# Weights decoded in tile pairs by three bit operations, with a late range check and a new order of the first three unit pairs

## The chip, the cores and the metric

The kernel runs on one core of a Trainium2 chip. The metric is the device time of one execution in microseconds. The engines are TensorE (PE, with its weight loads PEld), VectorE (DVE), ScalarE (ACT), GpSimd (POOL) and SyncE (SP), whose queue issues all transfers of this kernel.

## What is computed

A gated linear attention with a complex diagonal decay feeds a two-layer network. Shapes: batch 4, heads 8, sequence 768, head width 48; the network maps 3072 rows of 384 to 2048 and back.

```python
mag = sqrt(a_re**2 + a_im**2)
scale = minimum(mag, 0.999) / (mag + 1e-6)
a_re_n, a_im_n = a_re * scale, a_im * scale
for t in range(S):
    new_re = ar * S_re - ai * S_im
    new_im = ar * S_im + ai * S_re
    S_re, S_im = new_re + outer(k[t], v[t]), new_im
    y[t] = q[t] @ S_re
x = y.transpose(0, 2, 1, 3).reshape(B * S, H * D)
h = x @ w_in
out = (h - tanh(h)) @ w_out
```

All inputs are float32 but the two weight matrices, which arrive as float64 and lie in memory as 64-bit words.

## The kernel before, in words

The sequence is cut into 6 chunks of 128 positions. A unit is one batch entry in one chunk (24 units); a unit pair g (12 of them, two batch entries of one chunk) is what the network works on: 256 rows. Letters name the steps. Gates: B, b, C, D, E (`gates_b` to `gates_e`) turn the decays of a pair into scale factors and rotations, with Ln, Exp, Arctan and Sin on ACT. `p` (`products`) scales and rotates q and k of one unit, splits them into two f16 parts and has them transposed by a DMA (the first four units work in f32 and are transposed by PE). `a` (`attention`) is the unit's attention: scores, mask, the state Z, and at the end `x16`, which a DMA transposes into `xT`.

Network: `head(g, fp)` multiplies `xT` of pair g with two of the 16 column tiles of w_in (18 matmuls of 256 columns, L521), takes tanh on ACT and h − tanh(h) on DVE into `mt`. `split` writes it as two f16 parts into `mg`. `tail(g, fp)` multiplies these with two tiles of w_out (12 matmuls of 384 columns, L548) into two accumulators; after the eighth, ACT copies them into an `io` tile (L552) and a DMA writes the result. A tail follows its head by LAG = 4 heads; 8 heads make a stage.

Weights: `decode` (L172 to L191) loads one tile of 384 64-bit words per partition (384 KB) into one of four `io` buffers, views it as low and high 32-bit words, each with a step of 8 bytes, and builds from them a float32 with a shifted exponent in `wtmp`: DVE shifts the low word (L181), ACT multiplies the high word as a float by a power of two into the low word's place (L184, shown as L112), DVE merges sign and top exponent bit (L185) and the rest (L186). ACT copies it to f16 (`dechi`), DVE subtracts that for the low half (`declo`). This runs once for each of 32 tiles. `weight_stats` squares both high halves of a tile on ACT and sums them; `check_stats` at the end compares these sums and other statistics with limits, and a kernel in general arithmetic runs if one is broken. Helpers record most instructions, so they show L102 (and L112, L119) in the trace.

Order of the work: START is the list of steps before the first head; FIRST, SECOND and CYCLE list, for pair 0, pair 1 and all others, which step stands at which of 16 half-steps of a stage. `i3` decodes tile 3 of w_in, `o3` of w_out, `q0` loads q, k, v of a unit, `p2` is a piece of products of unit 2g + 2, `w0` the weight statistics. EARLY (pairs 0 and 1) and OFFSET (later) shift the priority of each kind of instruction; a scheduler at build time orders each engine's queue by priority among what is ready in its own model, and the engines then run their queues in order.

Of the kernel before, what the change touches and what calls it, by code (L numbers as in the profile page):

```python
# [11 lines left out]
I32 = mybir.dt.int32  # L12
# [74 lines left out]
def tile_fast(ctx: ExitStack, tc: tile.TileContext, flag, a_in, qkv_in, win_in, wout_in, sq_c, vec_c, lim_c, out):  # L87
# [30 lines left out]
    def combine(which, kind, **k):  # L118
        by_name[ENGINE[which]](kind).tensor_tensor(**k)  # L119
# [52 lines left out]
    def decode(ft, kinds=(0, 1)):  # L172
        for kind in kinds:
            src = (win_in, wout_in)[kind]
            raw = sb.tile([P, 2, DM], F32, name="io", bufs=BUFS["io"]).rearrange("p two n -> p (two n)").bitcast(I32).rearrange("p (n two) -> p n two", two=2)
            SP("dec").dma_start(out=raw, in_=src[:, ft].bitcast(I32).rearrange("p (n two) -> p n two", two=2))
            tmp = sb.tile([P, DM], I32, name="wtmp", bufs=BUFS["wtmp"])
            lo, hi = raw[:, :, 0], raw[:, :, 1]
            top = raw.rearrange("p n two -> p (n two)").bitcast(U8).rearrange("p (n e) -> p n e", e=8)[:, :, 3]
            if ENGINE[f"lsb{kind}"] == "V":  # L180
                V("dec").tensor_scalar(out=tmp, in0=lo, scalar1=29, scalar2=None, op0=ALU.logical_shift_right)  # L181
            else:
                A("dec").activation(out=tmp, in_=top, func=AF.Copy, scale=1.0 / 32, bias=-0.484375)
            copy("base", "dec", lo.bitcast(F32), hi.bitcast(F32), 2.0 ** (-112 + SW // 8))  # L184
            V("dec").scalar_tensor_tensor(out=tmp, in0=hi, scalar=-1073741824, in1=tmp, op0=ALU.bitwise_and, op1=ALU.bitwise_or)  # L185
            V("dec").scalar_tensor_tensor(out=tmp, in0=lo, scalar=3, in1=tmp, op0=ALU.logical_shift_left, op1=ALU.bitwise_or)  # L186
            w = tmp.bitcast(F32)
            t = const.tile([P, 2, DM], F16, name=f"w{kind}_{ft}")
            (wi, wo)[kind][ft] = t
            copy("dechi", "dechi", t[:, 0], w)  # L190
            combine("declo", "declo", out=t[:, 1], in0=w, in1=t[:, 0], op=ALU.subtract)  # L191
# [389 lines left out]
    def step(g, x):  # L581
# [241 lines left out]
```

## Time and profile before

| | us |
|---|---|
| median of 3 runs | 574.05 (572.24 to 576.78) |
| span of the profiled execution, first to last instruction | 575.1 |
| PE, DVE, ACT busy in it | 504.1, 474.7, 473.0 |

The profile shows one execution, whose page gives its span; no other time of that execution is given. Its span is 1.05 us above the median. Times in rows are us from the start of the span; durations of single instructions are ns where a row says mean.

### The profile page before, as it was taken

Reading aid. Unit: us, or ns where it says so; the run is one execution under the profiler, and the core shown is the slowest. Engines: PE = TensorE matmul, PEld = TensorE weight load, DVE = VectorE, ACT = ScalarE, POOL = GpSimd, SP = SyncE. Lnnn points to the kernel's source line nnn. Section 1 sums busy time; section 2 is a strip of 40 time slices with the busy share of each in tenths; the row PEclk is TensorE's granted clock in tenths of the full one; section 3 lists DMA queues with packets and bytes.
Section 4 is the critical chain, followed back from the end, with each engine's and each line's share of the span. In section 5 each row is a group of like instructions: output and inputs, shape, how many; then the busy total and the mean of one; then the engine's idle time right before and its main releaser. Section 6 shows DMA issues by size and latency. Waiting matters only on the chain.

```text
span 575.1 us, 12672 instructions
## 1 busy us (share of the span) xinstructions
PE 504.1 (88%) x5058; PEld 387.7 (67%) x5058; DVE 474.7 (83%) x806; ACT 473.0 (82%) x951; POOL 2.1 (0%) x8
## 2 busy tenths in 40 slices
PE   2336499987699998999998999999999999999995
PEld 0125387865467876877776777778778777777773
DVE  4898899978799898898997998998998989853331
ACT  6978889897997998998988998998989989553551
POOL 1000000000000000000000000000000000000000
PEclk9859589998799999999998999999999999999998
DMA  7757744409757368267285285293582652720001
GB/s 229 229 165 172 244 135 107 129 14 175 152 93 153 98 103 175 67 134 166 56 152 135 57 169 147 67 184 104 100 178 65 135 110 56 146 59 15 2 27 33
DMA packets 133902, 68.12 MB, mean 118 GB/s; under 512 B 119982, under 2 KB 123694, under 8 KB 133836
## 3 DMA queue, kind: packets, MB, share of 16 engines
q1 hardware_dynamic: 133836, 67.25, 50.0%
q8 instruction: 41, 0.67, 0.5%
q14 instruction: 25, 0.20, 0.1%
HBM read 36.76 MB, written 4.78 MB: 72 GB/s over the span
## 4 chain that ended last, share of the span: by engine, by line
PE 35%; ACT 27%; DVE 21%; DMA 8%; issue 7%; SPq 0%; ACTq 0%; DVEq 0%
PE h L521 11%; PE o L548 11%; PE att L102 9%; ACT L102 5%; ACT a_raw L102 4%; DMA qT<-q 4%; DVE qkf L390 3%; DVE g_t L102 3%; DVE qkv_raw L387 2%; ACT mt L102 2%; ACT mg L102 2%; DVE q L119 2%; ACT g_t L102 2%; DVE mg L102 2%; DVE mt L102 2%
## 5 line engine op out<-in xcount | busy, mean ns | idle before, releaser
L521 PE MATMUL h<-xT,w 128*128 128x256 f16 x1728 | 208.3, 274 | 11.2 <-DMA xT<-x 8.9
L548 PE MATMUL o<-w,mg 128*128 128x384 f16 x1152 | 205.6, 328 | 4.4 <-ACT io L102 2.9
L521 PEld LDWEIGHTS <-w 128*128 128x128 f16 x1728 | 168.2, 98 | 40.8 <-DMA xT<-x 7.2
L548 PEld LDWEIGHTS <-mg 128*128 128x128 f16 x1152 | 111.8, 98 | 69.6 <-issue 4.6
L102 DVE SCALAR_TENSOR_TENSOR mt<-h,mt 128x512 f32<-128x512 f32 x96 | 64.9, 685 | 25.9 <-ACT mt L102 25.8
L102 DVE SCALAR_TENSOR_TENSOR mg<-mt,mg 128x512 f16<-128x512 f32 x96 | 65.1, 686 | 16.1 <-ACT mg L102 15.8
L102 ACT ACTIVATE mg<-mt 128x512 f16<-128x512 f32 x96 | 58.8, 624 | 22.1 <-DVE mt L102 21.9
L102 ACT ACTIVATE mt<-h 128x512 f32<-128x512 f32 x96 | 55.2, 586 | 20.5 <-PE h L521 19.9
L102 ACT ACT_TABLE_LOAD x39 | 50.0, 1283 | 1.4 <-PEq L816 0.8
L102 PE MATMUL att<-qT,kT 96*128 96x128 f16 (+1 forms) x544 | 41.8, 231 | 3.1 <-DMA kT<-k 2.5
L390 DVE TENSOR_TENSOR qkf<-qkv_raw,g_trig 128x768 f32<-128x768 f32 x44 | 41.0, 950 | 0.0
L102 ACT ACTIVATE a_raw<-a_raw 128x768 f32<-128x768 f32 (+2 forms) x49 | 38.9, 796 | 0.5 <-DVE a_raw L102 0.5
L102 PEld LDWEIGHTS <-kT 96*128 96x128 f16 x480 | 30.2, 101 | 6.1 <-DMA kT<-k 3.1
L102 DVE TENSOR_TENSOR a<-af,a 128x512 f16<-128x512 f32 x40 | 27.3, 685 | 7.7 <-ACT a L102 7.5
L102 DVE TENSOR_TENSOR af<-att,sqc 128x512 f32<-128x512 f32 x40 | 27.3, 687 | 6.5 <-PE att L102 5.3
L102 ACT ACTIVATE a<-af 128x512 f16<-128x512 f32 x40 | 24.9, 623 | 3.7 <-DVE af L102 3.7
L102 DVE SCALAR_TENSOR_TENSOR g_t<-g_t,a_raw 128x768 f32<-128x768 f32 (+1 forms) x26 | 23.2, 894 | 2.3 <-ACT a_raw L102 2.3
L102 ACT ACTIVATE w<-wtmp 128x384 f16<-128x384 f32 x32 | 16.0, 514 | 8.4 <-DVE wtmp L186 8.4
L102 ACT ACTIVATE g_trig<-g_t 128x768 f32<-128x768 f32 (+1 forms) x26 | 20.3, 785 | 2.9 <-DVE g_t L102 2.2
L102 ACT ACTIVATE g_t<-att 128x384 f32<-128x384 f32 x24 | 10.7, 485 | 13.8 <-PE att L219 13.8
L119 DVE TENSOR_TENSOR q<-qkf,q 128x768 f16<-128x768 f32 x20 | 19.1, 955 | 3.5 <-ACT q L102 3.4
L102 PE MATMUL att<-sqc,qkf 128*96 128x128 f32 x32 | 7.0, 386 | 16.1 <-DVE qkf L390 15.7
(94 smaller groups left out, 706.7 us busy)
## 6 DMA issues: line engine op xcount, KB each, us to landing
qkv_raw<-in_qkv SPq DMA_DIRECT2D x24, 576.0 KB
a_raw<-in_a SPq DMA_DIRECT2D x22, 384.0 KB
io<-in_win SPq DMA_DIRECT2D x16, 384.0 KB
io<-in_wout SPq DMA_DIRECT2D x16, 384.0 KB
out_dram<-io SPq DMA_DIRECT2D x24, 192.0 KB
a_raw<-in_a SPq DMA_DIRECT2D x4, 192.0 KB
xT<-x SPq DMA_TRANSPOSE x24
hd<-hscr SPq DMA_DIRECT2D x20, 3.0 KB
```

What stands on the lines that cost most here:

```text
L102: return f(*a, **k)
L119: by_name[ENGINE[which]](kind).tensor_tensor(**k)
L387: V("prod").scalar_tensor_tensor(out=x, in0=vw(e), scalar=E_MAX, in1=x, op0=ALU.min, op1=ALU.mult)
L390: V("prod").tensor_tensor(out=f, in0=x[:, :, None].broadcast_to([P, H, 2, D]), in1=tg[:, :, sl].rearrange("p r (h d) -> p h r d", d=D), op ...
L521: T("h").matmul(h_ps[:, j].rearrange("p (two t) -> p two t", two=2), lhsT=wi[ft][:, wp, kt * P:(kt + 1) * P], rhs=xT[:, :, xp, kt, :], sta ...
L548: T("o").matmul(o_ps[tt][:, :DM], lhsT=gg[:, gp, j * 256 + tt * P:j * 256 + (tt + 1) * P], rhs=wo[ft][:, wp], start=(ft == 0 and n == 0), ...
```

## The change

`decode(kind, fp)` now loads and decodes two tiles at once (768 words per partition, 768 KB) into one of three `io` buffers of twice the size, with two `wtmp` buffers of twice the size. DVE shifts the high word left by 3 and masks it in one instruction, merges the two top bits, and merges the top three bits of the low word. ACT copies with a scale of 2^8 to f16, and the low half is one SCALAR_TENSOR_TENSOR on DVE. A new step, `range_check`, loads every pair again in the last two stages, masks four exponent bits of the high words, compares them by XOR with a constant, and takes the maximum. The sums of squares take every sixteenth column of one tile in two and move to stage 10. START, FIRST, SECOND, a new THIRD and CYCLE order the steps anew; LAG is 5; some priorities change.

```diff
-BUFS = {"io": 4, "wtmp": 4, ...
-LAG = 4
+BUFS = {"io": 3, "wtmp": 2, ...
+LAG = 5
 START = (
-    "q0 i3 F0 F1 i1 o7 p0 q1 B1 p1 i5 o3 i0 p0 p1 b1 p1 p0 a0 a0 o1 a1 a1 i7 E1 o4 a0 i8 a0 i6 i2 i10 i11 a1 o5 a1 C1 o2 i15 a0 o6 i4 D1 "
+    "q0 i1 i0 F0 o3 F1 p0 q1 p1 B1 i2 o1 p0 p1 b1 p1 p0 a0 a0 o0 a1 a0 a1 i3 E1 i4 o2 a0 i5 a1 "
+    "a1 C1 o5 a0 o6 i7 "
 FIRST =
-    "0:p2 0:o11 0:p2 0:o13 0:p2 0:o0 0:p3 0:a1 1:i13 1:a2 2:i9 3:o15 3:o12 4:a2 4:o9 4:p3 5:a2 5:B2 5:b2 6:p3 7:a2 8:C2 8:o10 8:a3 9:a3 9:i12 10:i14 11:a2 11:o8 11:a3 11:D2 12:o14 12:B3 13:b3 14:E2 14:a3 "
+    "0:D1 0:p2 0:p2 0:p2 0:p3 0:a1 0:i6 1:a2 3:o7 4:a2 4:p3 5:o4 5:a2 5:B2 5:b2 6:p3 7:a2 8:C2 8:a3 8:a2 9:a3 10:a3 10:E2 11:D2 13:B3 13:b3 13:a3 14:a3 "
 SECOND =
-    "... 2:a2 2:a2 3:a1 3:p2 3:a1 4:C2 4:p3 5:D2 ... 9:w0 ... 13:p4 14:a3 14:w1 "
+    "... 2:a2 2:a2 3:a1 3:a1 4:p3 5:p2 5:C2 5:D2 ... 12:p4 13:p4 15:a3 "
+THIRD = (as CYCLE but for the places of C2, D2 and some a and p)
 CYCLE =
-    "0:p2 1:p2 2:p3 3:p3 4:w0 4:p2 ... 13:a2 15:w1 "
+    "0:p2 0:p2 2:p3 3:p3 4:p2 ... 13:a2 "
+LATE =
+    "10:0:w0 10:2:w1 10:3:r13 10:4:w2 10:5:r14 10:6:r12 10:6:w3 10:7:r15 10:8:w4 10:10:w5 10:12:w6 10:14:w7 11:0:r0 11:1:r1 11:2:r2 11:3:r3 11:4:r4 11:5:r5 11:6:r6 11:7:r7 11:8:r8 11:9:r9 11:10:r10 11:11:r11 "
 OFFSET: xf -30 -> 100, mt 400 -> 1000, cum 0 -> 700, load 400 -> 200
 EARLY: zhi 1000 -> 100, alo -30 -> 700, kv 700 -> 2000, glo 30 -> 100, dechi 1000 -> 400, declo 4000 -> -30
-    "w": (2 * FT, 4.0, 2.0 ** 21.9),
+    "w": (FT, 0.25, 2.0 ** 21),
+    "r": (FT, 0.0, 0.0),
+    def decode(kind, fp):
+        raw = io_tile().bitcast(I32)
+        SP("dec").dma_start(out=raw, in_=weights(kind, fp))
+        raw = raw.rearrange("p (n two) -> p n two", two=2)
+        lo, hi = raw[:, :, 0], raw[:, :, 1]
+        tmp = sb.tile([P, 2 * DM], I32, name="wtmp", bufs=BUFS["wtmp"])
+        V("dec").tensor_scalar(out=tmp, in0=hi, scalar1=3, scalar2=0x3FFFFFFF, op0=ALU.logical_shift_left, op1=ALU.bitwise_and)
+        V("dec").scalar_tensor_tensor(out=tmp, in0=hi, scalar=-1073741824, in1=tmp, op0=ALU.bitwise_and, op1=ALU.bitwise_or)
+        V("dec").scalar_tensor_tensor(out=tmp, in0=lo, scalar=29, in1=tmp, op0=ALU.logical_shift_right, op1=ALU.bitwise_or)
+        w = tmp.bitcast(F32)
+        t = const.tile([P, 2, 2 * DM], F16, name=f"w{kind}_{fp}")
+        copy("dechi", "dechi", t[:, 0], w, float(2 ** SW))
+        V("declo").scalar_tensor_tensor(out=t[:, 1], in0=w, scalar=float(2 ** SW), in1=t[:, 0], op0=ALU.mult, op1=ALU.subtract)
+    def weight_stats(fp):
+        for w in (wi, wo):
+            A("guard").activation(out=junk()[:, :DM // 16], in_=w[2 * fp][:, 0, ::16], func=AF.Square, accum_out=stat("w"))
+    def range_check(i):
+        raw = io_tile().bitcast(I32)
+        SP("guard").dma_start(out=raw, in_=weights(i // (FT // 2), i % (FT // 2)))
+        tmp = sb.tile([P, 2 * DM], I32, name="wtmp", bufs=BUFS["wtmp"])
+        V("guard").tensor_scalar(out=tmp, in0=raw[high words], scalar1=0x78000000, scalar2=0x38000000, op0=ALU.bitwise_and, op1=ALU.bitwise_xor)
+        V("guard").tensor_reduce(out=stat("r"), in_=tmp, axis=mybir.AxisListType.X, op=ALU.max)
-        plan = (FIRST, SECOND)[g] if g < 2 else CYCLE
+        plan = ((FIRST, SECOND, THIRD)[g] if g < 3 else CYCLE) + tuple((i, x) for h, i, x in LATE if h == g)
```

## Rows read from the trace of the kernel before

**Rows 1.** The page's first table: busy us of each engine, its share of the span and its instructions, whole span.

```profile
PE 504.1 (88%) x5058; PEld 387.7 (67%) x5058; DVE 474.7 (83%) x806; ACT 473.0 (82%) x951; POOL 2.1 (0%) x8
```

**Rows 2.** The page's second table: busy tenths of each engine in 40 equal slices of 14.4 us: PE, DVE and ACT.

```profile
PE   2336499987699998999998999999999999999995
...
DVE  4898899978799898898997998998998989853331
ACT  6978889897997998998988998998989989553551
```

**Rows 3.** Busy us of each engine by stretch (start:end, length, then PE, PEld, DVE, ACT and POOL with their instructions; last the granted clock as a share of 2.4 GHz, the DMA share and GB/s).

```profile
11.00:70.00 59.00, 25.74 (x126) 18.38 (x126) 52.08 (x111) 49.93 (x107) 0.00 (x0) 0.73 0.69 199
70.00:118.00 48.00, 46.21 (x365) 37.67 (x366) 45.60 (x88) 41.84 (x80) 0.00 (x0) 0.94 0.44 124
118.00:151.00 33.00, 22.54 (x213) 17.42 (x211) 25.66 (x40) 27.43 (x51) 0.00 (x0) 0.89 0.53 109
151.00:505.00 354.00, 344.56 (x3798) 267.00 (x3798) 323.86 (x525) 318.44 (x642) 0.00 (x0) 0.99 0.56 119
505.00:562.00 57.00, 57.00 (x519) 43.04 (x517) 23.62 (x37) 27.80 (x61) 0.00 (x0) 1.00 0.09 26
```

**Rows 4.** The chain of waits of two stretches, summed by line as shares of the stretch: first 0 to 75 us, then 118 to 151 us.

```profile
by line: PE att L102 15.2%; DMA qkv_raw<-in_qkv 8.8%; issue 6.9%; ACT io L112 6.5%; ACT w L102 5.9%; DVE w L102 4.6%; ACT L102 4.0%; DVE g_t L102 3.9%; DVE wtmp L185 3.7%; ACT g_trig L102 3.7%; DVE wtmp L186 3.5%; DMA xT<-x 3.4%; ACT a_raw 
...
by line: DMA kT<-k 14.9%; ACT L102 11.7%; ACT mt L102 7.7%; ACT a_raw L102 7.3%; ACT g_trig L102 7.3%; PE att L102 7.2%; issue 4.6%; ACT k L102 4.4%; ACT g_t L102 4.1%; ACT g_ep L102 3.7%; ACT junk L102 3.4%; ACT g_en L102 3.4%; PE att L219
```

**Rows 5.** The chain of waits over the whole span, in order of time (start us, us, what): the first feed-forward matmul, the same piece of two successive stages, and the last output copy.

```profile
70.16 1.89 PE h L521 x8
...
233.19 1.97 PE h L521 x18
...
272.77 1.97 PE h L521 x18
...
567.86 0.98 ACT io L102 x2
```

**Rows 6.** Groups of equal instructions over the whole span (line, engine, operation, out<-in, shape, count | busy us, mean ns | idle before them): the weight decoding and the squares of the weights.

```profile
L185 DVE SCALAR_TENSOR_TENSOR wtmp<-io,wtmp 128x384 int32<-128x384 int32 x32 | 17.5, 550 | 0.2
L102 DVE TENSOR_TENSOR w<-wtmp,w 128x384 f16<-128x384 f32 x32 | 17.2, 552 | 3.0 <-ACT w L102 2.8
L186 DVE SCALAR_TENSOR_TENSOR wtmp<-io,wtmp 128x384 int32<-128x384 int32 x32 | 17.2, 550 | 0.6 <-ACT io L112 0.6
...
L112 ACT ACTIVATE io<-io 128x384 f32<-128x384 f32 x32 | 16.7, 549 | 0.9 <-DVE wtmp L181 0.9
...
L102 ACT ACTIVATE junk<-w 128x384 f16<-128x384 f16 x32 | 16.5, 515 | 0.1
L102 ACT ACTIVATE w<-wtmp 128x384 f16<-128x384 f32 x32 | 16.0, 514 | 8.4 <-DVE wtmp L186 8.4
...
L181 DVE TENSOR_SCALAR wtmp<-io 128x384 int32<-128x384 int32 x32 | 10.8, 352 | 0.2 <-DMA io<-in_win 0.2
...
L102 ACT ACTIVATION_READ_ACCUMULATOR junk<-w 128x1 f32 x32 | 6.2, 193 | 0.0
```

**Rows 7.** The same view for shapes that lie near the new operations.

```profile
L102 DVE SCALAR_TENSOR_TENSOR g_t<-g_t,a_raw 128x768 f32<-128x768 f32 x22 | 20.9, 952 | 1.5 <-ACT a_raw L102 1.5
...
L102 DVE SCALAR_TENSOR_TENSOR a_raw<-a_raw,a_raw 128x768 f16<-128x768 f32 x10 | 9.6, 958 | 0.3
...
L102 ACT ACTIVATE a_raw<-a_raw 128x768 f16<-128x768 f32 x10 | 8.3, 828 | 0.0
...
L102 ACT ACTIVATE rawsq<-qkv_raw 128x144 f32<-128x144 f32 x24 | 7.5, 312 | 2.2 <-DMA qkv_raw<-in_qkv 1.2 <-DVE stats L102 1.0
...
L102 DVE TENSOR_REDUCE stats<-rawsq 128x3 f32<-128x144 f32 x24 | 7.1, 296 | 0.9 <-ACT rawsq L102 0.9
```

**Rows 8.** Busy us of DVE in the decoding, before and after 70 us: the lines L181, L185, L186 and the subtractions that write `w`, in this order, two stretches each.

```profile
0.00:70.00 70.00, 7.59 (x22) 0.77 0.70 207
70.00:118.00 48.00, 3.26 (x10) 0.94 0.44 124
...
0.00:70.00 70.00, 11.87 (x22) 0.77 0.70 207
70.00:118.00 48.00, 5.65 (x11) 0.94 0.44 124
...
0.00:70.00 70.00, 11.24 (x21) 0.77 0.70 207
70.00:118.00 48.00, 5.95 (x11) 0.94 0.44 124
...
0.00:70.00 70.00, 11.26 (x21) 0.77 0.70 207
70.00:118.00 48.00, 5.99 (x11) 0.94 0.44 124
```

**Rows 9.** The list in order of time of DVE at the end (start us, us, engine, line, operation): the statistics check.

```profile
561.37 0.68 DVE L102 TENSOR_TENSOR af<-stats,af 128x219 f32<-128x219 f32 x2
562.09 0.61 DVE L102 TENSOR_REDUCE okm<-af 128x1 f32<-128x438 f32 x1
```

**Rows 10.** What the DMA queue of SP waited for before 70 us (us in total, times, longest us), and one of its issues from the list in order of time (start us, us).

```profile
SPq L176 <- DVE wtmp L186: 20.8, 8, 4.4
...
67.59 1.24 SPq L485 DMA_TRANSPOSE xT<-x  x1
```

More of the change, by code (lines that the diff above doesn't have):

```diff
@@ L53 @@
+    "13:p4 15:a3 "
+).split()))
+THIRD = tuple((int(i), x) for i, x in (y.split(":") for y in (
+    "0:p2 1:C2 2:p3 3:p3 4:p2 5:a2 5:p3 5:D2 5:a2 6:a3 6:a2 7:a2 8:a3 9:a3 10:B3 10:a2 10:a3 10:a3 11:E2 11:b3 13:a2 "
 ).split()))
 CYCLE = tuple((int(i), x) for i, x in (y.split(":") for y in (
-    "0:p2 1:p2 2:p3 3:p3 4:w0 4:p2 5:C2 5:p3 5:D2 5:a2 5:a2 6:a3 7:a2 7:a2 8:a3 9:a3 10:B3 10:a2 10:a3 10:a3 11:E2 11:b3 13:a2 15:w1 "
+    "0:p2 0:p2 2:p3 3:p3 4:p2 5:C2 5:p3 5:D2 5:a2 5:a2 6:a3 7:a2 7:a2 8:a3 9:a3 10:B3 10:a2 10:a3 10:a3 11:E2 11:b3 13:a2 "
@@ L56 @@
 ).split()))
-OFFSET = {"gate": 2000, "gatep": 700, "prod": 0, "prodp": -100, "qkhi": -30, "vhi": -30, "vlo": 1000, "zhi": 100, "zlo": -300, "S": 30, "af": -300, "ahi": -30, "alo": -2000, "qu": 0, "y": 0, "xf": -30, "kv": 2000, "z": 100, "guard": -2000, "h": 0, "tanh": -2000, "mt": 400, "ghi": 2000, "glo": -30, "o": 0, "out": -100, "dec": -100, "dechi": 100, "declo": 200, "table": -30, "cum": 0, "load": 400}
-EARLY = {"gate": 2000, "gatep": 100, "prod": 0, "prodp": 0, "qkhi": -30, "vhi": 0, "vlo": -2000, "zhi": 1000, "zlo": -300, "S": 100, "af": 1000, "ahi": -700, "alo": -30, "qu": 0, "y": 4000, "xf": 0, "kv": 700, "z": 200, "guard": -700, "h": 0, "tanh": 30, "mt": 400, "ghi": 100, "glo": 30, "o": 0, "out": 700, "dec": 0, "dechi": 1000, "declo": 4000, "table": -300, "cum": 0, "load": 0}
+LATE = tuple((int(g), int(i), x) for g, i, x in (y.split(":") for y in (
+    "10:0:w0 10:2:w1 10:3:r13 10:4:w2 10:5:r14 10:6:r12 10:6:w3 10:7:r15 10:8:w4 10:10:w5 10:12:w6 10:14:w7 11:0:r0 11:1:r1 11:2:r2 11:3:r3 11:4:r4 11:5:r5 11:6:r6 11:7:r7 11:8:r8 11:9:r9 11:10:r10 11:11:r11 "
+).split()))
@@ new lines @@
+OFFSET = {"gate": 2000, "gatep": 700, "prod": 0, "prodp": -100, "qkhi": -30, "vhi": -30, "vlo": 1000, "zhi": 100, "zlo": -300, "S": 30, "af": -300, "ahi": -30, "alo": -2000, "qu": 0, "y": 0, "xf": 100, "kv": 2000, "z": 100, "guard": -2000, "h": 0, "tanh": -2000, "mt": 1000, "ghi": 2000, "glo": -30, "o": 0, "out": -100, "dec": -100, "dechi": 100, "declo": 200, "table": -30, "cum": 700, "load": 200}
+EARLY = {"gate": 2000, "gatep": 100, "prod": 0, "prodp": 0, "qkhi": -30, "vhi": 0, "vlo": -2000, "zhi": 100, "zlo": -300, "S": 100, "af": 1000, "ahi": -700, "alo": 700, "qu": 0, "y": 4000, "xf": 0, "kv": 2000, "z": 200, "guard": -700, "h": 0, "tanh": 30, "mt": 400, "ghi": 100, "glo": 100, "o": 0, "out": 700, "dec": 0, "dechi": 400, "declo": -30, "table": -300, "cum": 0, "load": 0}
@@ L170, in tile_fast @@
     wi, wo = {}, {}
[L172 to L191, printed above, removed]
@@ L193, in weight_stats, with io_tile, weights @@
-    def weight_stats(ft):
-        A("guard").activation(out=junk()[:, :DM], in_=wi[ft][:, 0], func=AF.Square, accum_out=stat("w"))
-        A("guard").activation(out=junk()[:, :DM], in_=wo[ft][:, 0], func=AF.Square, accum_out=stat("w"))
+    def io_tile():
+        return sb.tile([P, 4 * DM], F32, name="io", bufs=BUFS["io"])
+    def weights(kind, fp):
+        return (win_in, wout_in)[kind][:, 2 * fp:2 * fp + 2].rearrange("p f n -> p (f n)").bitcast(I32)
+    def decode(kind, fp):
[11 more added lines that the diff above has]
+        V("declo").scalar_tensor_tensor(out=t[:, 1], in0=w, scalar=float(2 ** SW), in1=t[:, 0], op0=ALU.mult, op1=ALU.subtract)
+        for j in range(2):
+            (wi, wo)[kind][2 * fp + j] = t[:, :, j * DM:(j + 1) * DM]
@@ new lines, in weight_stats @@
+    def weight_stats(fp):
[5 more added lines that the diff above has]
+        tmp = sb.tile([P, 2 * DM], I32, name="wtmp", bufs=BUFS["wtmp"])
+        V("guard").tensor_scalar(out=tmp, in0=raw.rearrange("p (n two) -> p n two", two=2)[:, :, 1], scalar1=0x78000000, scalar2=0x38000000, op0=ALU.bitwise_and, op1=ALU.bitwise_xor)
+        V("guard").tensor_reduce(out=stat("r"), in_=tmp, axis=mybir.AxisListType.X, op=ALU.max)
@@ L549, in tail @@
         if fp == FT // 2 - 1:
-            o_sb = sb.tile([P, 2, DM], F32, name="io", bufs=BUFS["io"])
+            o_sb = io_tile()[:, :2 * DM].rearrange("p (two n) -> p two n", two=2)
             for tt in range(2):
@@ L587, in step @@
         elif kind in "io":
-            decode(i, (0,) if kind == "i" else (1,))
+            decode(0 if kind == "i" else 1, i)
         elif kind == "w":
-            if 1 <= g <= FT // 2 and (kind, 2 * g + i) not in live:
-                live[kind, 2 * g + i] = True
-                weight_stats(2 * (g - 1) + i)
+            weight_stats(i)
+        elif kind == "r":
+            range_check(i)
         elif kind in "pa":
```

4 lines of the change are left out of this document (2 added, 2 removed).

## The prediction

> **What bounds the kernel now.** Read the page's table of engines first, then the slices, then stretches, then the chain. By the table PE is busy 88% of the span, DVE 83%, ACT 82% [rows 1]: an average over stages with different limits. The slices show where they differ: PE is poorly filled in the first five slices, dips again in the tenth and eleventh, and is full from the twelfth on; DVE and ACT are full almost from the start and thin out only at the end [rows 2]. The table by stretches says it in us [rows 3]:
>
> - 11 to 70: PE 25.74 of 59.00 us, DVE 52.08, ACT 49.93. Nothing of the feed-forward part runs; the two elementwise engines are the limit, and TensorE works at a granted 0.73, a mixture of its two levels, 1.2 and 2.4 GHz.
> - 70 to 118: PE 46.21 of 48.00, DVE 45.60, ACT 41.84: all three are full.
> - 118 to 151: PE 22.54 of 33.00, DVE 25.66, ACT 27.43: nobody is full, a chain of waits runs through ACT and one transposing DMA (14.9% of that stretch) [rows 4].
> - 151 to 505: PE 344.56 of 354.00. PE is the limit.
> - 505 to 562: PE 57.00 of 57.00, with DVE at 23.62 and ACT at 27.80.
>
> So what the change takes from DVE and ACT after 151 is worth at most the 9.4 us that PE idles there, and what it takes before 151 is worth what sits on the chain. In the chain up to 75 us, the lines of the weight decoding hold 6.5% (ACT, `io`), 5.9% (ACT, `w`), 4.6% (DVE, `w`), 3.7% and 3.5% (DVE, `wtmp`) [rows 4]: 24.2% of 75 us, 18.2 us. The first feed-forward matmul (L521) starts at 70.16 [rows 5]. The decoding is no filler there; it stands in two in-order queues in front of what the first feed-forward matmul needs.
>
> **The change, part by part.** *Decode on DVE.* Now a tile costs 352 + 550 + 550 + 552 ns on DVE [rows 6], a pair of tiles 4.01 us, all 32 tiles 64.1 us. After it a pair costs one TENSOR_SCALAR of 768 columns, two bitwise SCALAR_TENSOR_TENSOR of 768 and one SCALAR_TENSOR_TENSOR for the low halves. Those of 768 columns with one f32 result took 952 ns, with f16 958 [rows 7]. The TENSOR_SCALAR with two operations has no row. From below: the one-operation form took 352 ns at 384 columns where the two-source forms took 550, half the time per column, so 768 columns are worth about 0.55; from above, if the second operation costs it that advantage, 0.95. I take 0.55, since its nearest row reads the same 8-byte step. A pair is then 0.55 + 0.95 + 0.95 + 0.96 = 3.41 us, 16 pairs 54.6: 9.5 us less on DVE (3.1 less with 0.95).
>
> *Decode on ACT.* Now 549 + 514 ns a tile [rows 6], 34.0 us in all. After it one copy of 768 columns to f16 for a pair, 828 ns [rows 7]: 13.2 us. 20.8 us less. The wait of DVE for the ACT copy in the middle of the bit operations goes too; late next is DVE's own third operation.
>
> *What that is worth up to the first feed-forward matmul at 70.* Of the 18.2 us on the chain 9.3 are ACT's (12.4%) and 8.9 DVE's. ACT's fall by 61% (13.2 for 34.0), 5.7 us; DVE's by 15%, 1.3 us. Against it: START now holds 13 of the 16 pairs, 44.3 us of DVE, where the trace has 7.59 + 11.87 + 11.24 + 11.26 = 42.0 us of decoding before 70 [rows 8]. That may cost its 2.3 us. Bounds: a gain of 12 (the 9.3 of ACT and the rest of DVE's share), a loss of 2. I take −6.
>
> *70 to 118.* DVE holds 3.26 + 5.65 + 5.95 + 5.99 = 20.9 us of decoding there [rows 8]; after the change three pairs, 10.2 us. PE is full already, so the chain gains at most PE's 1.8 idle us: −1, bounds −2 and 0.
>
> *118 to 151.* PE idles 10.5 us here because the gates and products of the next units come late from DVE and ACT. With 10 us less decoding on DVE in the stretch ahead, and E2 placed at half-step 10 of FIRST instead of 14, they come earlier. Bounds: −10.5 (all idle time goes) and +3 (D1 now stands behind START instead of in it, and its three 768-column ACT operations, 0.83 us each by the nearest row [rows 7], come later by one head). I take half: −5.
>
> *151 to 505.* The sums of squares of weights leave ACT: 32 of 515 ns with a read of 193 ns [rows 6], 22.7 us, 2.8 us in each of eight stages of 39.6 us (233.19 to 272.77 on the chain) [rows 5]. PE covers that. Worth it are only those waits in which PE stands behind ACT; of 9.4 us PE idle I take −2, bounds −6 and +2 (`cum`, `mt`, `xf`, `load` change their priority, LAG becomes 5 with the same five `mg` buffers: either sign).
>
> *The late checks.* 16 squares of 24 columns: no row is that short; the nearest, 144 columns, took 312 ns [rows 7], with its read about 0.5 us, 8 us of ACT in 57 us where ACT is free for 29. The range check costs DVE 16 times a TENSOR_SCALAR of 768 (0.55 to 0.95) and a TENSOR_REDUCE of 768. The reduces took 296 ns at 144 columns [rows 7] and 610 at 438 [rows 9], a slope of 1.07 ns a column, so 768 come to 0.96 us. Together 24 to 31 us, 12 of the 16 pieces in the last stage. DVE is idle for 33.4 us in 505 to 562 [rows 3], so PE's steady work hides it; the reloads, 16 of 768 KB, meet a DMA share of 0.09. Without that cover, when the last reduce ends after 562, the check of the statistics, now 561.37 to 562.70 [rows 9], would slide behind the output copy that follows PE's last matmul at 567.86 [rows 5]: I take 0, bounds 0 and +8.
>
> **Sum.** −6 −1 −5 −2 +0 = −14 on a profiled span of 575.1, 561.1. The median of the runs, 574.05, stands 1.05 below that span (the runs reach from 572.24 to 576.78, so about 1% is what a measurement can tell): 560.0 us. The outer ends of the terms together are −30 and +15, but they will not all meet: 550 to 569 is the range of this case alone.
>
> **Rivals.**
>
> *ACT was the real limit of the start.* Then the whole 20.8 us come off, with 1.4 us of the squares that run before 151, and the −2 later: 574.05 − 24 = 550. For it: the chain between 118 and 151 runs through ACT lines; against it: DVE is the busier one between 11 and 118 (97.7 to 91.8 us) [rows 3] and gives up only 9.5.
>
> *DVE stays the limit and nothing comes earlier.* START's 13 pairs hold DVE for 44.3 us, not less than the 42.0 of now, the first matmul stays at 70, PE stays full to 118, and only part of the 118 to 151 hole closes: −3, 571. For it: DVE's 52.08 of 59 us. Against it: decode has a low urgency, so critical operations pass it wherever the schedule lets them.
>
> *The weight loads block SP (slower).* SP issues in order and waits for weight buffers: 20.8 us in 8 waits before 70, the longest 4.4 [rows 10], with the loads of `qkv_raw` and the transposes of `x` behind them (the last of the two `xT` that open the first stage is issued at 67.59) [rows 10]. After the change there are 3 buffers instead of 4, each with twice the bytes, and each is held until the third bit operation (2.45 us after landing at best). `q1` now stands behind 2.3 MB of weights instead of 1.2: at 199 GB/s [rows 3] 5.8 us later. If SP then waits twice for a pair in front of each `xT`, twice 4.4, the first matmul comes at 70 + 5.8 + 8.8 and the gains of the start are lost: 574.05 + 14.6 − 5 = 584. It decides from the point where these delays exceed the 14 us of the sum. Against it: DMA has a third of its time free, and a pair's load has fewer, longer pieces.
>
> *The 8-byte step halves the bit operations.* If a stream that skips every second word moved at half rate, a bit operation on 768 columns would cost what 1536 dense ones cost: from 550 and 952 ns for 384 and 768 [rows 6, 7], 1.76 us, and a pair 0.95 + 1.76 + 1.76 + 0.96 = 5.4, 23 us more DVE instead of 9.5 less, all of it ahead of the stages that PE limits, less the 7 us that the ACT share gives back there: about 590. Against it: L185 reads `hi` with this step and took 550 ns, the dense `w` subtraction 552 [rows 6]. [...]
>
> **How the numbers follow.** Chances: the sum 0.52, ACT as the limit 0.20, nothing earlier 0.16, SP blocked 0.09, half rate 0.03. The time is the likeliest case's, 560.0. The range reaches down to 546, past the ACT case by the runs' scatter, and up to 575, past "nothing earlier"; beyond it lie the two slow cases and a few per cent below. Faster by over 1% (under 568.3): the sum without its upper edge and the ACT case, 0.72. Within 1%: "nothing earlier" and that edge, 0.18. Slower: 0.10.
>
> **What would show it.** Right: bit operations of 0.55, 0.95, 0.95 us, 0.96 for the low half, 0.83 for the ACT copy; the first feed-forward matmul between 58 and 68 instead of 70.16; less than 7 us of PE idle in the 33 us that follow PE's first full stretch; stages of 39.6 us in the middle as before; reduces of 0.96 us that end ahead of PE's last matmul. Wrong: a first feed-forward matmul at 70 or later, a first bit operation of 0.95, SP waiting on weight buffers for more than the 20.8 us of now before it, or PE gaps in the last two stages behind reduces.

## The result, and the profile after

The kernel after takes 583.64 us (median of 4 runs, 582.17 to 584.72) against 574.29 us of the kernel before in the same comparison: a ratio of 1.0147 [1.0105, 1.0188]. The forecast was 560.0 us, faster; it is slower by 1.5%. The profiled execution took 582.17 us, its span is 580.3 us. In all comparisons here the time of a profiled execution stands 1.7 to 1.9 us above its span; by that the profile before, of 575.1 us, is of an execution of about 577 us (an estimate), at the upper end of its runs, while the profile after is of the lowest of its four, so that the spans differ by 5.2 us where the medians differ by 9.35.

The page of the kernel after: busy us of each engine, and its slices of 14.5 us (PE, DVE, ACT), which answer to [rows 1, 2].

```profile
PE 506.0 (87%) x5058; PEld 387.0 (67%) x5058; DVE 491.6 (85%) x774; ACT 448.1 (77%) x870; POOL 1.9 (0%) x8
...
PE   2367499969998989999999999999899899899995
...
DVE  4899999877998978988979989989889988977861
ACT  6948399887987968969969979879789788654450
```

ACT gave up 24.9 us (473.0 to 448.1) and the span still grew. PE's row of nines now has eights in its second half. The same stretches as [rows 3], put at the kernel after's own stages:

```profile
11.00:67.00 56.00, 26.48 (x129) 19.40 (x130) 51.62 (x75) 37.40 (x73) 0.00 (x0) 0.85 0.70 222
67.00:115.00 48.00, 47.32 (x376) 37.78 (x375) 44.80 (x65) 42.27 (x71) 0.00 (x0) 0.96 0.37 107
115.00:148.00 33.00, 25.90 (x283) 20.67 (x282) 26.06 (x42) 27.08 (x47) 0.00 (x0) 0.84 0.65 142
148.00:505.00 357.00, 336.27 (x3677) 258.45 (x3675) 319.09 (x516) 302.45 (x589) 0.00 (x0) 1.00 0.58 123
505.00:564.00 59.00, 58.68 (x541) 44.59 (x539) 44.23 (x68) 29.87 (x74) 0.00 (x0) 1.00 0.58 191
```

The hole behind PE's first full stretch has shrunk from 10.5 to 7.1 us, where the prediction named less than 7. In the long middle, where DVE and ACT are both less busy than before, PE now idles 20.7 us instead of 9.4.

The stage is the unit in which to follow this. The start of the first feed-forward matmul of each pair, in us, read from the list of PE's instructions (a stage is the difference of two neighbours):

| pair | 0 | 1 | 2 | 3 | 4 | 5 | 6 | 7 | 8 | 9 | 10 | 11 | end |
|---|---|---|---|---|---|---|---|---|---|---|---|---|---|
| before | 70.2 | 118.5 | 173.3 | 210.7 | 251.8 | 291.4 | 334.0 | 373.6 | 413.2 | 453.0 | 491.9 | 529.0 | 575.1 |
| after | 66.6 | 115.4 | 162.7 | 204.4 | 247.0 | 288.5 | 330.8 | 372.3 | 414.7 | 455.7 | 495.4 | 532.3 | 580.3 |
| lead | 3.6 | 3.1 | 10.6 | 6.3 | 4.8 | 2.9 | 3.2 | 1.3 | -1.5 | -2.7 | -3.5 | -3.3 | -5.2 |

The kernel after leads by 10.6 us when pair 2 starts, gives back 4.3 us of this in pair 2's own stage, and the rest and more in the later ones, 1 to 3 us in most of them. The median stage from pair 2 to pair 10 is 41.5 us; it was 39.6. Pieces of the chain (start us, us, what) that answer to [rows 5]:

```profile
66.60 9.16 PE h L540 x62
...
330.79 2.13 PE h L540 x18
...
368.28 3.94 DMA xT<-x
372.26 2.12 PE h L540 x18
...
573.10 0.98 ACT io L111 x2
```

From 330.79 to 372.26 is 41.47 us, and what stands on the chain directly ahead of the first head is the transposing DMA of x. What PE waited for from 225 to 480 us, and what SP waited for before 70 us (us in total, times, longest), the latter against [rows 10]:

```profile
PE h L540 <- DMA xT<-x: 8.1, 6, 1.8
```

```profile
SPq L189 <- DVE wtmp L195: 23.9, 6, 5.8
```

In the kernel before PE waited for `xT` not once in this stretch; it waited 6.4 us for `a_raw` of ACT there, where the kernel after waits 3.5 us for `a_raw` and 2.0 for `z` of DVE. The new operations, and the shortened squares (line, engine, operation, shape, count | busy us, mean ns | idle before them), against [rows 6, 7]:

```profile
L111 DVE TENSOR_REDUCE stats<-wtmp 128x1 f32<-128x768 int32 x16 | 15.2, 950 | 0.4
L195 DVE SCALAR_TENSOR_TENSOR wtmp<-io,wtmp 128x768 int32<-128x768 int32 x16 | 15.2, 949 | 0.1
L194 DVE SCALAR_TENSOR_TENSOR wtmp<-io,wtmp 128x768 int32<-128x768 int32 x16 | 15.1, 951 | 0.1
...
L111 DVE SCALAR_TENSOR_TENSOR w<-wtmp,w 128x768 f16<-128x768 f32 x16 | 15.0, 950 | 0.0
...
L111 ACT ACTIVATE w<-wtmp 128x768 f16<-128x768 f32 x16 | 13.3, 837 | 8.6 <-DVE wtmp L195 8.6
...
L111 DVE TENSOR_SCALAR wtmp<-io 128x768 int32<-128x768 int32 x16 | 8.9, 555 | 6.4 <-DMA io<-in_win 3.9 <-DMA io<-in_wout 2.5
...
L193 DVE TENSOR_SCALAR wtmp<-io 128x768 int32<-128x768 int32 x16 | 8.8, 552 | 0.8 <-DMA io<-in_win 0.5 <-DMA io<-in_wout 0.3
...
L111 ACT ACTIVATE junk<-w 128x24 f16<-128x24 f16 x16 | 3.9, 241 | 0.4
...
L111 ACT ACTIVATION_READ_ACCUMULATOR junk<-w 128x1 f32 x16 | 3.0, 186 | 0.0
```

DVE at the end, in order of time, against [rows 9]: the last reduce of the range check and the end of the check of the statistics.

```profile
562.96 0.95 DVE L111 TENSOR_REDUCE stats<-wtmp 128x1 f32<-128x768 int32 x1
...
566.74 0.61 DVE L111 TENSOR_REDUCE okm<-af 128x1 f32<-128x438 f32 x1
```

The check of the statistics ends at 567.35, 5.8 us ahead of the last output copy at 573.10. So the prices of the new operations were right (the shortened square with its read took 0.43 us for the "about 0.5" of the prediction), the start is earlier, and the checks do not make the end later; the loss is made in the middle stages.

### The profile page after: what moved, and what is told of

It reads as the page before. It is cut to its first block, busy times and chain, and to the rows that moved or that the text cites. A ratio compares the mean times of both kernels' runs of the same rounds, so it can differ in the third digit from the quotient of the medians.

```text
span 580.3 us, 12580 instructions
## 1 busy us (share of the span) xinstructions
PE 506.0 (87%) x5058; PEld 387.0 (67%) x5058; DVE 491.6 (85%) x774; ACT 448.1 (77%) x870; POOL 1.9 (0%) x8
## 4 chain that ended last, share of the span: by engine, by line
PE 48%; ACT 15%; DVE 15%; DMA 14%; issue 6%; SPq 1%; ACTq 0%; DVEq 0%
PE h L540 19%; PE o L567 15%; PE att L111 10%; DMA xT<-x 6%; DMA kT<-k 3%; ACT a_raw L111 3%; ACT L111 2%; DVE qkf L409 2%; DMA qT<-q 2%; DVE g_t L111 2%; PE att L482 2%; DVE qkv_raw L406 1%; DVE a_raw L111 1%; DVE mg L111 1%; PE att L235 1%
## 5 line engine op out<-in xcount | busy, mean ns | idle before, releaser
L111 PE MATMUL att<-qT,kT 96*128 96x128 f16 (+1 forms) x544 | 42.4, 230 | 7.9 <-DMA kT<-k 7.3
L111 ACT ACTIVATE q<-qkf 128x768 f16<-128x768 f32 x20 | 16.8, 840 | 13.1 <-DMA qT<-q 12.9
L111 ACT ACTIVATE w<-wtmp 128x768 f16<-128x768 f32 x16 | 13.3, 837 | 8.6 <-DVE wtmp L195 8.6
L128 DVE TENSOR_TENSOR k<-qkf,k 128x768 f16<-128x768 f32 x20 | 19.0, 950 | 0.5 <-ACT k L111 0.5
```

The lines of the kernel that those rows point to most:

```text
L111: return f(*a, **k)
```

## The experiments

**What lengthens the middle stages?** Three parts of the change act there beside the squares that went: A, the later tail (LAG 5 with the five `mg` buffers of before); B, the changed priorities of OFFSET; and C, the new order of THIRD and CYCLE. First each was undone by itself in the kernel after, then all three.

From pair 2 to pair 10, single stages stand 2.1 to 4.7 us above the median stage of their trace (in the kernel before pair 5, 42.6 beside 39.6). In each of these the granted clock over the stage is 0.96, where it is 1.00 in nearly all others. In h1_xf, h2_mt and h4_load below, whose middle stages are otherwise those of the kernel before, pair 5 took 42.8 us at 0.96, and 41.2 and 41.1 us at 1.00: about 1.6 us that come and go between executions. In the kernel after no stage from pair 2 to pair 10 has it; its 41.5 us are at 1.00. So medians of stages are compared below, not single ones.

*e1_lag4*

```diff
-LAG = 5
+LAG = 4
```

> The changed kernel with LAG back at 4. Seen so far: its first feed-forward matmul and stage 2 start 4 to 11 us earlier than before, but six stages from 204 to 456 take 41.5 us or more instead of 39.6, because the first head waits for xT, whose f16 copy of x stands in ACT's queue behind the gates. Theory A (a tail that follows five heads later with five mg buffers makes each split wait for a tail, which pushes ACT's order back): stages return to 39.6, time about 583.6 - 15 = 569. Theory B (the changed priorities made ACT's order): stages stay at 41 to 42, time 580 to 584. Theory C (the new places of the steps in CYCLE made it): same as B here.

586.66 us, 1.0231 [1.0186, 1.0275]. The stages are 41.1 to 42.6 from pair 2 to pair 8, but for one of 45.0 (clock 0.96). A alone falls.

*e2_prio*

```diff
-OFFSET: xf 100, mt 1000, cum 700, load 200
+OFFSET: xf -30, mt 400, cum 0, load 400
```

> The changed kernel with the later stages' priorities (OFFSET: xf, mt, cum, load) back at the values of before. Theory B: the copy of x stands ahead of the gates again, stages of 39.6, time about 569. Theories A and C: stages stay at 41 to 42, 580 to 584.

578.59 us, 1.0065 [1.0032, 1.0098]: 5 us less than the kernel after. Four stages read 40.2 to 40.5; three stand at 42.4 to 43.4, at a clock of 0.96 (the profiled execution took 582.41 us, above the median). B alone brings part of the loss back, not the 15 us that its theory asked for.

*e3_cycle*

```diff
-THIRD, CYCLE as after
+THIRD = CYCLE = "0:p2 1:p2 2:p3 ..." (the order of before without w0, w1)
```

> The changed kernel with THIRD and CYCLE both as CYCLE was before, without the squares of the weights. Theory C: stages of 39.6, about 569. Theories A and B: 41 to 42, 580 to 584.

582.09 us, 1.0144 [1.0107, 1.0180], stages 41.3 to 42.4 from pair 4 to pair 7, PE's waits for `xT` 7.2 us from 225 to 480. The order alone is not it: C alone falls.

*e4_all3* (the three edits together)

> LAG 4, OFFSET and CYCLE (also for the third pair) of before together, in the changed kernel: what stays of the change are the pair decode, START, FIRST, SECOND, EARLY, the late checks, and the missing squares. If any of A, B, C or a mixture holds: stages of 39.6 and the gain of the start kept, 560 to 570. If the missing squares of the weights (2.8 us of ACT a stage that the scheduler filled in) or the pair decode itself made the stages longer: 41 to 42 a stage still, 580 to 584.

575.62 us (10 runs, 572.62 to 581.96), 1.0017 [0.9985, 1.0049]; the median stage from pair 2 to pair 10 is 40.2 (two stand at 43.2 and 43.4, clock 0.96), and from 225 to 480 no wait for `xT` is left. The start keeps its gain (pair 2 at 163.2), and yet the kernel is only as fast as before.

**The parts alone, from the other side.**

*f1_decode*: the kernel before with the pair decode and its buffers, everything else as it was (START and FIRST name a pair where its first tile stood).

```diff
-def decode(ft, kinds=(0, 1)): ...
+def decode(kind, fp): ... (as after)
-BUFS io 4, wtmp 4
+BUFS io 3, wtmp 2
```

> The kernel before with the pair decode alone: two tiles at once, three bit operations, three io and two wtmp buffers; START and FIRST as before with each pair at the place of its first tile; LAG, EARLY, OFFSET, CYCLE and the sums of squares as before, no range check. Theory D (the decode gives the start its gain and does not touch the stages that PE limits): stage 2 starts about 10 us before 173, stages of 39.6, time 574.5 - 10 = 564. Theory E (the shifted end of the start, or the pair decode itself, changes the later queues): the lead at stage 2 is eaten by stages of 40 to 42, time 570 to 580.

575.95 us, 1.0012 [0.9985, 1.0040]: nothing gained. ACT falls from 49.93 to 41.20 us between 11 and 70, as the prediction wanted, but DVE only from 52.08 to 51.23, and the first head starts at 70.8. The chain of this kernel ahead of it (start us, us, what):

```profile
62.46 5.02 DMA io<-in_win
...
68.06 0.88 DVE vv L391
...
70.99 5.01 PE h L522 x39
```

A load of 768 KB stands on this chain, but it costs only what DVE waits for it. That wait, from the list in order of time, and what PE waited for between 55 and 75 us, first here, then in the kernel before:

```profile
67.50 0.56 DVE L184 TENSOR_SCALAR wtmp<-io 128x768 int32<-128x768 int32 x1 [0.42 <-DMA io<-in_win]
```

```profile
PE att L102 <- DVE qkf L391: 6.5, 1, 6.5
```

```profile
PE h L521 <- DMA xT<-x: 7.0, 1, 7.0
```

The load costs DVE 0.42 us. PE waits 6.5 us for a product (`qkf`) out of DVE's queue, which its own queue needs ahead of the head here. What is late next is DVE, as the rival "DVE stays the limit and nothing comes earlier" had it.

*f2_prio_alone*: the kernel before with the new OFFSET only (the edit of e2 reversed).

> The kernel before with the new OFFSET alone (xf 100, mt 1000, cum 700, load 200 from stage 2 on). Theory B (these priorities cost the middle stages about 1 us each, as e2 shows the other way round): stages 3 to 9 of 40.5 to 41.5 and 580 to 584. If they cost only together with LAG 5 or with the missing squares: stages of 39.6 and 574.

585.92 us, 1.0181 [1.0136, 1.0227]. Pair 2 starts at 173.2 as before; then the stages are 41.2 to 42.5 (pair 4 to pair 7), and from 225 to 480 PE waits 3.1 us for `xT` and 4.3 us for `z` of DVE. Four numbers cost 12.0 us (573.89 in this comparison) in a kernel that is otherwise untouched: B holds, from both sides.

*f5_prio_cycle*: the kernel after with the old OFFSET and the old order, LAG 5.

> The changed kernel with OFFSET and CYCLE (also for the third pair) of before, LAG still 5. If LAG 5 with five mg buffers costs by itself: slower than e4's 575.6, about 578 to 580. If LAG does nothing once the priorities are back: 575 to 576. LAG 4 alone (e1) made the changed kernel slower, so 5 may even help: 572 to 574.

575.89 us, 1.0025 [1.0001, 1.0049]: with e4 (575.62) this says that LAG is worth nothing here.

**Where the rest is.** Stages of 40.2 in e4 and f5 stand against 39.6 of before, and what is left that differs in the middle is the decode with its buffers, and that ACT has *less* to do: no squares. With the new decode and buffers alone (f1) the stages are 39.6, so the squares are next.

*f4_squares*: e4 with the full squares at their old places, from pair 1 on, instead of the short late ones.

```diff
-weight_stats: [:, 0, ::16] of one tile in two, in LATE
+weight_stats: [:, 0] of every tile; SECOND and CYCLE with w0, w1 as before
```

> e4 (LAG 4, OFFSET and CYCLE of before in the changed kernel) with the sums of squares of the weights back at their places and size of before; the range check stays late. e4 had stages of 40.2 where before has 39.6, and lost 9 of its 10 us of lead after stage 2. Theory F (the squares held the order of ACT's queue in place): stages of 39.6, time about 569. Rival (the rest sits in SECOND, EARLY or the first stages' order): stages of 40.2, about 575.

573.87 us, 0.9990 [0.9957, 1.0024]: the stages from pair 4 to pair 8 are 39.6 to 40.3 again (one is 42.9, clock 0.96), while the stage of pair 1 grew from 47.6 to 53.4.

*g1_squares_mid*: the same squares, a stage later (pairs 2 to 9), none in SECOND.

> e4 (the changed kernel with LAG 4, OFFSET and CYCLE of before) with the full sums of squares in stages 2 to 9 at CYCLE's places, none in SECOND. Theory F (the squares keep the order of the middle stages, and f4 lost 6 us because two of them stood in SECOND): stage 2 starts at 163 as in e4, stages of 39.6, time 574 - 8 = 566. Rival (the lead at stage 2 is given back whatever the middle looks like, because the first stages leave work undone): stage 3 and 4 long, 572 to 575.

569.13 us (567.03 to 572.47), 0.9906 [0.9868, 0.9943]: faster than both kernels. Pair 2 starts at 165.0, the stages from pair 3 to pair 8 are 39.6 to 40.4 but for one (42.7, clock 0.96). Theory F holds, within about 3 us of its 566. From 225 to 480 us the wait of PE that differs between e4 and g1 is that of the matmuls which sum the decays' logarithms, first e4, then g1:

```profile
PE att L238 <- ACT a_raw L111: 9.2, 6, 2.8
```

```profile
PE att L238 <- ACT a_raw L111: 5.5, 6, 1.9
```

So with 15.8 us more work on ACT (16.5 + 6.2 in [rows 6] for 3.9 + 3.0) ACT's gate results come earlier relative to PE's queue. From the start of pair 2 to that of pair 11 PE idles 9.5 us in g1 and 15.4 in e4, 5.9 of the 7.2 us by which this stretch is shorter. That the orders built differ is seen; why the build-time scheduler places them so was not traced.

*g2_lag5*: g1 with LAG 5.

> The same with LAG 5. If five mg buffers throttle a lag of five: 2 to 4 us slower than with LAG 4. If the lag is only a matter of which wait the scheduler sees: equal within 2 us.

578.61 us, 1.0060 [1.0028, 1.0092]: 9.5 us more than g1. The stage of pair 2 takes 44.4 us (PE waits 3.0 us for `kT` and 2.4 for `xT` in it), another 42.9, both at a clock of 0.96. Neither forecast holds; in e4 against f5 the same number was worth nothing.

*g3_old_decode*: g1 with the tile-by-tile decode of before, four `io` and four `wtmp` buffers, no range check.

> g1 with the old decode (tile by tile, four io and four wtmp buffers, each pair's two tiles at the pair's place) and without the range check. Theory G (the gain of the start comes from the new order of START, FIRST, SECOND and EARLY, since f1 with the decode alone gained nothing): first feed-forward matmul within 2 us of g1's, stage 2 within 3 us, time within 3 us of g1. My prediction's step (the decode's smaller load on ACT and DVE is the gain): stage 2 about 10 us later than in g1, time 574 to 578.

575.80 us, 1.0018 [0.9995, 1.0040]. The first head comes at 60.5, but the stage of pair 0 takes 64.7 us: PE idles 11.3 of the 65 us from 60 to 125. Of this 2.8 us are waits for halves of weights, and the longest are for `mg`, the split of tanh's difference,

```profile
PE o L571 <- ACT mg L110: 4.5, 2, 2.3
...
PE h L544 <- ACT w L110: 2.0, 1, 2.0
PE h L544 <- DVE w L110: 0.8, 1, 0.8
```

and pair 2 starts at 172.7, which fits the second forecast. At the first head 17 of the 32 tiles are decoded here and 20 in g1. Within the new order the new decode is worth 6.7 us by g1, 5.8 by g4 below, which like g3 has no range check; in the old order (f1) it was worth nothing, and the new order without it nothing either.

*g4_no_check*: g1 without the range check (that test of the weights is left out).

> g1 without the range check and its 16 reloads. If it is hidden by PE as predicted: within 1 us of g1. If the reloads or the reduces delay the last stages: 2 to 4 us faster than g1, in stages 9 to 11.

569.99 us, 0.9917 [0.9887, 0.9947], against 569.13 with it: the check is hidden.

**Which priority?** Each of the four alone in the kernel before.

*h1_xf, h2_mt, h3_cum, h4_load*

```diff
-"xf": -30   -"mt": 400    -"cum": 0     -"load": 400     (one of them per kernel)
+"xf": 100   +"mt": 1000   +"cum": 700   +"load": 200
```

> The kernel before with one priority changed alone: xf from -30 to 100 (the attention output's last operations and its transposing DMA rank later). Theory: this key is the one that delays the transpose behind the gates and makes the middle stages 41.3 us long instead of 39.6; then it alone gives most of the 11.9 us that all four keys cost, 582 to 587, and PE waits for xT for over 10 us from 225 to 480. Rival: another key (mt, cum or load) does it, and this run is 573 to 577 with stages of 39.6.

> The kernel before with mt alone from 400 to 1000 (tanh's difference and its f16 copies rank later). Theory (xf is the cause): 573 to 577, stages 39.6. Rival (mt is the cause: the split halves reach the tails late, PE waits for mg): 580 or more with stages over 41.

> The kernel before with cum alone from 0 to 700 (the matmuls that sum the decays' logarithms rank later on PE). Theory (xf is the cause): 573 to 577, stages 39.6. Rival (cum is the cause: the gates start late, so all of ACT's gate work stands later and in front of the attention output): 580 or more with stages over 41.

> The kernel before with load alone from 400 to 200 (loads of q, k, v and of decays rank earlier on SP's queue). Both theories: 573 to 577, stages 39.6, because these loads land long before their use in the middle stages; 580 or more would say that their place on SP's queue delays the transposes.

| | us | ratio |
|---|---|---|
| h1_xf | 574.30 | 0.9998 [0.9972, 1.0024] |
| h2_mt | 574.16 | 1.0012 [0.9989, 1.0036] |
| h3_cum | 586.67 | 1.0218 [1.0177, 1.0260] |
| h4_load | 573.34 | 0.9995 [0.9971, 1.0020] |

The theory written down (xf) falls; `cum` alone gives the whole loss of f2. It is a priority on PE, of a few short matmuls, and it moves another engine's queue. ACT in the kernel before, where the f16 copy of the attention's output stands among the gates (start us, us, engine, line, operation), with the DVE instruction that makes `xf` and the transposing DMA:

```profile
282.38 0.55 DVE L102 SCALAR_TENSOR_TENSOR xf<-att,xf 128x384 f32<-128x384 f32 x1
...
283.91 0.51 ACT L102 ACTIVATE x<-xf 128x384 f16<-128x384 f32 x1
284.33 0.56 ACT L102 ACTIVATE g_ep<-att,vec 128x384 f32<-128x384 f32 x1
...
285.49 1.22 SPq L102 DMA_TRANSPOSE xT<-x  x1
```

The same in h3_cum:

```profile
286.81 0.55 DVE L102 SCALAR_TENSOR_TENSOR xf<-att,xf 128x384 f32<-128x384 f32 x1
...
287.97 0.56 ACT L102 ACTIVATE g_ep<-att,vec 128x384 f32<-128x384 f32 x1
...
291.66 0.52 ACT L102 ACTIVATE x<-xf 128x384 f16<-128x384 f32 x1
...
293.56 2.02 SPq L102 DMA_TRANSPOSE xT<-x  x1
297.04 2.14 PE L521 MATMUL h<-xT,w 128*128 128x256 f16 x18 [0.43 <-DMA xT<-x]
```

`xf` is ready at 282.93 and copied at 283.91 in the one; it is ready at 287.36 and copied at 291.66 in the other, behind all four g_ep and g_en and two a_raw. That is 3.3 us more, and the transpose, for which PE did not wait before, now ends 0.43 us after PE wants it. That is only a part of the loss. What PE waited for from 225 to 480 us (us in total, times, longest), in the kernel before and in h3_cum (there beside 5.9 us for `a_raw`):

```profile
PE att L219 <- ACT a_raw L102: 6.4, 7, 1.9
```

```profile
PE att L102 <- DVE z L102: 4.2, 6, 0.7
PE h L521 <- DMA xT<-x: 3.7, 6, 1.2
```

The wait for `z` is that of the moved matmuls themselves: of four that ran in one row before, two now stand behind DVE's update of the state (at 286.35 they start 0.72 us late behind `z`). In the stage of pair 6, at clock 1.00 in both, 39.6 us become 41.4, and PE's idle time 0.4 us becomes 1.6, 0.71 of it for `z` and 0.51 for `xT`. In the kernel after `xT` is the larger of the two, 8.1 to 2.0. It has the order of h3 on ACT:

```profile
236.40 0.56 ACT L111 ACTIVATE g_ep<-att,vec 128x384 f32<-128x384 f32 x1
...
240.61 0.52 ACT L111 ACTIVATE x<-xf 128x384 f16<-128x384 f32 x1
```

and g1, with `cum` at 0, that of before:

```profile
236.68 0.51 ACT L111 ACTIVATE x<-xf 128x384 f16<-128x384 f32 x1
237.10 0.56 ACT L111 ACTIVATE g_ep<-att,vec 128x384 f32<-128x384 f32 x1
```

*i1_cum0*: the kernel after with `cum` at 0 and nothing else.

> The kernel after with cum alone back at 0; xf, mt and load stay at their new values, LAG at 5, the orders new, no squares in the middle. Theory (cum at 700 is what the new priorities cost): the same as the kernel after with all four old values, 578.6, that is 576 to 581, with stages of 40.2 to 40.5. Rival (the cost is cum's only beside the old order, and in the new one another key or their combination carries it): 582 to 586 with stages of 41.4 as in the kernel after.

577.19 us, 1.0045 [1.0013, 1.0076], stages of 40.0 from pair 4 to pair 7: 6.4 us of the loss, and no less than e2 gained with all four keys (578.59). `cum` is what the new priorities cost in the kernel after too.

## Why the prediction was wrong, point by point

By its own terms, read off the table of stages:

| term | forecast | measured |
|---|---|---|
| to the first head | -6 (-12 to +2) | -3.6 |
| pair 0's stage (70 to 118) | -1 (-2 to 0) | +0.5 |
| pair 1's stage (with the hole 118 to 151) | -5 (-10.5 to +3) | -7.5 |
| middle (151 to 505; here pair 2 to pair 11) | -2 (-6 to +2) | +13.9 |
| end | 0 (0 to +8) | +1.9 |
| sum on the span | -14 | +5.2 |

The medians differ by 9.35 us, 4 more than these two spans; h4_load, with the middle stages of the kernel before, takes 353.7 us from pair 2 to pair 11 where the trace of before takes 355.7.

- *The prices of the operations: right*, all five that the prediction listed within 0.02 us. The two-operation TENSOR_SCALAR took 552 ns, the lower bound that was chosen. The rival in which the 8-byte step halves the bit operations is dead: 951 and 949 ns where it asked for 1.76 us.
- *The start: right in sum* (-10.6 for -12 when pair 2 starts), *but by luck in part, and not for the reason given.* The first head gains less than forecast and pair 1's stage more, and the two nearly cancel. Other traces of the same first stages (e1 to e4, f5, g2, i1) have pair 2 at 162.4 to 164.7, and those with the first stages of before (f2, h1 to h4) at 170.1 to 173.2, so that the gain is rather 9 (an estimate from their middles). The prediction took the decode's share of the chain and scaled it down, 5.7 of the 7 us for ACT. f1 shows that this alone gains nothing: ACT is busy 8.7 us less between 11 and 70, and PE waits for DVE. g3 shows that the order alone brings the first head to 60.5 and loses it again in pair 0's stage. Only the order that loads the pairs early, with a decode cheap enough to keep up, gives the gain. Of the 6.2 us by which the kernel after issues the transpose of x ahead of the first head earlier, the transpose itself takes 2.6 back. On the chains, before first:

```profile
67.59 2.52 DMA xT<-x
```

```profile
61.39 5.17 DMA xT<-x
```

  Between 62 and 67 us the DMA share of the kernel after is 1.03, between 67.5 and 70 that of before 0.38; that the larger loads beside it are what slows the transpose was not tested.
- *The other two rivals of the start.* ACT was not the limit: between 11 and 67 us it is busy 37.40 us and DVE 51.62, and the head comes 3.6 us earlier, not 20.8. That DVE holds everything back is what f1 shows in the old order; in the new order the head came earlier all the same.
- *SP blocked by the loads: its sign came, its price did not.* SP waited 23.9 us for `wtmp` before 70 us (21.0 before its own first head), over the 20.8 named as the point of doubt, and the first head was still 3.6 us earlier. This rival's 584 lies next to the 583.64 measured by luck: it put the loss ahead of the first head, and it arose in the middle.
- *The late checks: right* (shown in g1 against g4, where LAG is 4). The last reduce ends at 563.9, 9 us ahead of the last copy, and g4 gives the price as nothing within 1 us. The +1.9 at the end is one more tail behind the last head (LAG 5); the last stage takes 48.0 us in all traces with LAG 5 but one of 48.2, and 45.8 to 46.2 in those with LAG 4.
- *The middle: the step that failed.* It reads "worth it are only those waits in which PE stands behind ACT; of 9.4 us PE idle I take -2, bounds -6 and +2", with the four priorities named as "either sign". The gain was bounded by a row, the +2 by none, and the sign "stages of 39.6 us in the middle as before" failed: they are 41.5 us. Two things stood in its place. The priority `cum` alone costs 12.9 us in the kernel before (h3, 586.67 against 573.73) and 6.4 us in the kernel after (i1). And taking the squares from ACT, priced at a small gain, is no gain: with the old order, priorities and LAG the median stage is 40.2 without the squares and 39.6 with them, 575.62 against 569.13 us (e4, g1).

From the kernel after to the best version, by medians: `cum` back 583.64 to 577.19; the other three keys and the cycle's order 577.19 to 575.89 (f5); LAG 575.89 to 575.62 (e4); full squares in pairs 2 to 9, 575.62 to 569.13 (g1). The second and third of these steps are within the runs' scatter. Between g1 and the forecast 9 us remain: its pair 2 starts 3.7 us later than the 161.3 that the first three terms ask for, and its middle takes 357.9 us, 2.2 more than before instead of 2 less; the rest is the distance of medians, spans and the last stage.

What stays open: why the squares' absence makes the built order worse, and why LAG 5 costs 9.5 us in g2, 0.3 in f5 against e4 and gains 3 in the kernel after against e1. Both are seen as other orders of the queues; no run isolates the instruction that decides.

## What to carry to other kernels

Where a scheduler at build time orders in-order queues, a changed priority has no price of its own: price it by what stands behind what in the built queues, keep its bound as wide as a loss in every stage makes it (here 12.9 us, under 2 in each), and try each key alone, since one number of four carried the loss here and the other three, alone in the kernel before, nothing. A chain shows a load in its whole length (5.02 us in f1), even where the engine waits for its last 0.42 us only: read the wait beside it. Before scaling down an engine's share of a chain, name what is late next, here the other engine's queue, and ask whether the order lets it come earlier. Work that is removed from an engine with slack moves its neighbours too (the median stage here is 40.2 us without ACT's squares in it and 39.6 with them): compare the stage length, not the busy time.

## What the runs showed of the hardware

- A TENSOR_SCALAR with two integer operations on 768 columns of int32 with an 8-byte step took 552 ns, and 555 with AND and XOR; the two-source forms took 950, and a TENSOR_REDUCE by maximum over 768 int32 also 950.
- A square with its sum over 24 columns costs 241 + 186 ns on ACT where 384 columns cost 515 + 193 [rows 6]: for a sixteenth of the columns 60% of the time.
- The granted clock had two levels: in windows of 0.5 us the traces of the kernels before and after read 1.00 or 0.50, but for the windows in which one follows the other. In the kernel before, from start to start on PE, 4608 columns of matmul took 1.95 us at 1.00 (249.82 to 251.77) and 768 took 0.64 us at 0.50 (308.00 to 308.64): 2.36 and 1.20 columns a ns.
- A gap of PE had a lower granted clock behind it in some executions and not in others. In g1, in the stage of pair 5 (columns as in [rows 3]), PE idles 1.6 us of three, and the granted clock of the next six us is 0.78 and 0.66, a mixture of 1.00 and 0.50, though PE is nearly full in them (2.73 and 3.00 us of three):

```profile
296.00:299.00 3.00, 1.36 (x13) 1.07 (x11) 2.57 (x5) 2.97 (x4) 0.00 (x0) 1.00 1.02 224
299.00:302.00 3.00, 2.73 (x24) 2.00 (x24) 2.92 (x6) 1.80 (x5) 0.00 (x0) 0.78 0.66 111
302.00:305.00 3.00, 3.00 (x29) 2.67 (x27) 1.95 (x4) 2.02 (x4) 0.00 (x0) 0.66 0.63 242
```

  That stage takes 42.7 us beside its neighbours' 39.6: 1.9 us of idle time (0.4 in the neighbours) and, as an estimate from these shares, 3 x 0.22 + 3 x 0.34 = 1.7 us of clock. In h2_mt the same wait, 2.06 us in the stage of pair 5, is followed by a clock of 1.00, and the stage takes 41.2 us:

```profile
303.00:306.00 3.00, 2.44 (x29) 1.94 (x29) 2.92 (x6) 1.80 (x5) 0.00 (x0) 1.00 0.64 105
```
